# A gated mix of sliding-window attention and a routed expert: the written order of all five engines exchanged for another

## The chip, the cores and the metric

The kernel runs on one core of a Trainium2 chip. The metric is the time of one execution on the device in microseconds (us); the time of a kernel is the median of its runs.

The core's engines work side by side, each through its own list of instructions in order: TensorE (PE, matmuls; PEld is its weight load), ScalarE (ACT), VectorE (DVE), GpSimd (POOL) and SyncE (SP), whose list here is nothing but DMA issues. They wait for each other on semaphores.

## The reference

Input x is 2048 rows of 512 (bfloat16). It is used three times and mixed:

```python
g = _sigmoid((x * gate_w).sum(-1, keepdims=True))
# a: 32 heads of 16; row i sees rows i-255 .. i
mask = (idx[:, None] - idx[None, :] >= 0) & (idx[:, None] - idx[None, :] < W)
a = softmax(where(mask, q @ k.T * Dh ** -0.5, -1e9)) @ v, heads joined, @ wo
# b: the 8 rows of largest x @ w_r go through a gated network of width 1792
y = (_silu(x_sel @ w_gate) * (x_sel @ w_up)) @ w_down * sigmoid(r_sel)
b = x, with y added at the 8 rows
return g * a + (1 - g) * b
```

(The lines of a and b are put together from the reference's; q, k, v come from x @ wqkv.)

## The kernel before

**Tiling.** Heads go in four groups c = 0 to 3 of eight heads (128 columns). For each group `proj` makes Q, K and V of each quarter tc of the rows (512 rows) on PE: eight matmuls over half the contraction each, four on one half of the array and four on the other (L628; the first quarter of group 0 uses the whole array, L621). `q_tail`, `k_tail` and `v_tail` bring them out of PSUM: a cast (L575) on DVE or ACT; for K four products with a head mask into `Kbd` (L587), for V a transpose (L603) and two products into `Vbd` (L607).

**Units.** The scores are made in 156 units (`unit`): 128 of four matmuls (two blocks of 32 keys) and 28 of sixteen (L658), on two PSUM banks in turn. One exponential on ACT per unit (L669) writes the probabilities into the ring `PT`, and one small product with a triangle mask (L680), on DVE or POOL, cuts the edge. `pv` multiplies probabilities and V for 128 rows (L699; one operation is eight matmuls of 34 columns), in batches of up to four blocks of rows that share the PSUM tile `psO`. `norm` ends a batch: reciprocal (L726), scale by g (L738), product (L742) into `On`, then a transposing DMA into `OT` (L772), or, in the two last batches, a transposing matmul (L759) and a copy (L764 on ACT, L767 on DVE). Only then may the next batch write `psO`.

**Output.** `outp(a)` multiplies 128 rows of `OT` by wo (L793, tail L790), adds (1 - g) * b (L798; the last block on ACT, L796) and sends them out (L801).

**Expert.** `z_item`, `router`, `ffn` and `ffd` make the gate, find the eight rows, and put them through the network (L873, 112 matmuls of 8 columns; L915). Their weights come by DMA in 35 pieces, each gated on one exponential.

**End.** Three DVE operations test the first 480 columns of the reciprocals `RC` (L1041, L1042, L1043), three more the last 32; a matmul sums the results (L1048), DVE writes `flag` (L1051), every engine loads it (L1181) and branches (L1183) past a general path that is there for other inputs.

**The order.** Nothing of the order follows from the text of these functions. `add` and `dma` only collect operations, numbered as they come; `Sched.schedule` then takes each engine's list from `ORDER` (the gated weight pieces have negative numbers), and an operation that may run on two engines (`alt`) runs on the one whose list it stands in. `BANK` says for each PSUM item which of the two `psG` banks it takes, and which half of the array comes first. `FILL` puts idle matmuls ahead of a unit: a value under 16 is that many pairs on `psO`, which wait for the last norm; 17 and 33 are one matmul on bank 0 or 1 of `psG`. `emit` works out the semaphores from the dependences.

Numbers that the steps below use:

| number | operation |
|---|---|
| 0, 65 to 74 | zero operand of the first idle matmuls (L458), and those ten (L534) |
| 15, 16, 17 | load of the first columns of wk, wq, wv (L489) |
| 24, 25, 26 | transposing load of XT rows 0-383, 384-511, 512-1023 (L483) |
| 18 to 21 | permutation of the first V weights (L495) |
| 75-78, 84-87 | K of rows 0-127, Q of rows 0-383 |
| 79, 80-83 | the cast of that K, its four Kbd pieces |
| 553 to 566 | first half of the expert's network (L873) |
| 1696, 1697, 1698 | last norm |
| 1710, 1721, 1728, 1737 | output sums 12, 13, 14 and 15 |
| 1670, 1699; 1671, 1700 | the transposing matmuls of the two last batches; their copies |
| 1739-1741, 1742-1744 | test of 480 columns of RC, of the last 32 |
| 1745, 1746 | sum of the tests on PE, flag |

Of the kernel before, what the change touches and what calls it, by code (L numbers as in the profile page):

```python
# [39 lines left out]

FILL = {}
FILLN = 240
ORDER = {}
BANK = ""

# [15 lines left out]
class Sched:  # L61
# [64 lines left out]
    def add(self, eng, fn, r=(), w=(), due=0.0, occ=100.0, lat=None, half=2, cls="", item=None, ss=None, nm=1, cw=0, alt=None):  # L126
# [4 lines left out]
        if eng == "pe":  # L131
            op.cw = float(cw)
            op.so = max(1.03 * occ, 0.834 * cw * (2 if half in (0, 1) else 1))
            if ss is not None:
                op.fill = FILL.get(self.nfill, 0)
                self.nfill += 1
# [211 lines left out]
def fast_path(nc, sem_es, flag, A_x, A_wqkv, A_wo, B_x, B_w_r, B_w_gate, B_w_up, B_w_down, gate_w, out):  # L348


    with ExitStack() as es:
# [706 lines left out]
        if SHOW is not None:  # L1058
# [44 lines left out]
FILL = {15: 2, 18: 1, 39: 1}  # L1103
BANK = ("2020230020200202202000222030202200220022000202022202000022002222002022002")
ORDER = {
# [40 lines left out]
    "act": [16, 22, 23, 15, 88, 93, 104, 13, 114, 122, 119, 129, 157, 160, 169, 172, 151, 185, 201, 215, 224, 227, 286, 236, 248, 251, 260, 263, 276, 295,   # L1146
# [929 lines left out]
```

## Time and profile before

| | |
|---|---|
| median of 3 runs (lowest, highest) | 181.54 us (181.53, 181.98) |
| the profiled execution | 182.41 us |
| its span, first to last instruction | 179.8 us |
| mean granted PE clock | 0.971 |
| HBM read, written | 11.81 MB, 4.20 MB |

The span begins with loads and tables until the first projection at 7.8 us; from 11.9 to 167 us the exponentials run; the last output product ends at 172.8 us, and the flag and the branch close the span. A row of the chain of waits or of the timeline has its start and its length in us, then the engine, the line and the tiles; a group has busy time, the mean of one in ns, and the idle time of the engine ahead of it with what ended it.

### The profile page before, as it was taken

How to read it: one execution, taken by the hardware profiler on the slowest of the kernel's cores; microseconds unless marked ns; L12 is line 12 of the kernel's file. 1: busy time of each engine (PE TensorE's matmuls, PEld its weight loads, DVE VectorE, ACT ScalarE, POOL GpSimd, SP SyncE). 2: the span in 40 equal slices, each digit the busy share in tenths (PEclk: the TensorE clock that was granted, in tenths of full speed). 3: DMA queues.
4: the chain of work that ended last, by engine and by line, in shares of the span. 5: the costliest groups of instructions: out<-in, count | busy, mean ns of one | idle time of the engine just before them, and what ended most of it. 6: DMA issues, size and time to landing. Idle time of an engine off the chain costs nothing.

```text
span 179.8 us, 10017 instructions
## 1 busy us (share of the span) xinstructions
PE 156.8 (87%) x4568; PEld 109.7 (61%) x4568; DVE 123.4 (69%) x343; ACT 137.6 (77%) x168; POOL 73.0 (41%) x118
## 2 busy tenths in 40 slices
PE   5599997999979989899888999699999989979850
PEld 1245674877556686675566658378768667856520
DVE  7075999898486539565765868577796785657760
ACT  2056988999988968888878959799999988957120
POOL 2052078992937476334525317633135336001000
PEclk9969999999999996999999999999999999999996
DMA  4994061656563574634451412120231025546420
GB/s 99 217 216 114 12 188 36 135 134 147 122 157 106 150 122 139 146 107 114 129 117 57 117 36 62 55 71 4 60 93 33 5 54 156 155 129 113 145 88 16
DMA packets 35745, 18.68 MB, mean 104 GB/s; under 512 B 27616, under 2 KB 35568, under 8 KB 35568
## 3 DMA queue, kind: packets, MB, share of 16 engines
q1 hardware_dynamic: 34560, 17.71, 41.2%
q8 instruction: 36, 0.59, 1.4%
q10 hardware_dynamic: 1072, 0.26, 0.7%
q14 instruction: 13, 0.11, 0.2%
q0 software_dynamic: 64, 0.02, 0.0%
HBM read 11.81 MB, written 4.20 MB: 89 GB/s over the span
## 4 chain that ended last, share of the span: by engine, by line
PE 63%; issue 10%; ACT 10%; DVE 10%; DMA 3%; SPq 1%; POOL 0%; POOLq 0%; DVEq 0%
PE f_psO L699 19%; PE f_psG L628 17%; PE f_psS L658 16%; ACT f_PT L669 9%; PE f_psG L793 5%; DMA f_XT<-in_A_x_dram 3%; DVE f_On L742 2%; PE f_psG L621 2%; PE f_psG L873 2%; PE f_psG L915 2%; DVE f_RC L726 1%; DVE f_PT L523 1%; DVE f_RG L738 1%; DVE f_VT L603 1%; SPq L483 1%
## 5 line engine op out<-in xcount | busy, mean ns | idle before, releaser
L669 ACT ACTIVATE f_PT<-f_psS 128x1024 bf16<-128x1024 f32 (+3 forms) x156 | 133.0, 917 | 20.6 <-PE f_psS L658 19.7
L658 PE MATMUL f_psS<-f_QT,f_Kbd 64*128 64x256 bf16 (+3 forms) x960 | 65.9, 225 | 4.2 <-issue 2.2
L699 PE MATMUL f_psO<-f_Vbd,f_PT 64*128 64x34 bf16 x2880 | 60.8, 174 | 5.5 <-issue 2.7
L680 POOL TENSOR_TENSOR f_PT<-f_PT,f_MK 128x128 bf16<-128x128 bf16 (+1 forms) x65 | 38.0, 593 | 65.1 <-ACT f_PT L669 62.2
L699 PEld LDWEIGHTS f_psO<-f_Vbd,f_PT 64*128 64x128 bf16 x2880 | 55.5, 93 | 14.2 <-DVE f_On L742 4.8
L628 PE MATMUL f_psG<-f_XT,f_W 64*128 64x512 bf16 x360 | 62.7, 380 | 0.1
L658 PEld LDWEIGHTS f_psS<-f_QT,f_Kbd 64*128 64x128 bf16 x960 | 32.4, 94 | 21.6 <-ACT f_PT L669 6.0
L680 DVE TENSOR_TENSOR f_PT<-f_PT,f_MK 128x128 bf16<-128x128 bf16 (+1 forms) x91 | 22.3, 271 | 6.5 <-ACT f_PT L669 6.2
L628 PEld LDWEIGHTS f_psG<-f_XT,f_W 64*128 64x128 bf16 x360 | 20.6, 94 | 8.5 <-PE f_psG L628 0.5
L793 PE MATMUL f_psG<-f_wo,f_OT 64*128 64x512 bf16 x112 | 21.2, 376 | 0.0
L587 POOL TENSOR_SCALAR f_Kbd<-f_Kr,f_hm 128x512 bf16<-128x512 bf16 (+2 forms) x11 | 16.2, 1479 | 12.1 <-DVE f_W L495 7.6
L587 DVE TENSOR_SCALAR f_Kbd<-f_Kr,f_hm 128x512 bf16<-128x512 bf16 (+2 forms) x57 | 20.1, 378 | 1.3 <-ACT f_Kr L575 1.1
L607 POOL TENSOR_SCALAR f_Vbd<-f_VT,f_pb 128x512 bf16<-128x512 f32 x17 | 12.7, 750 | 14.3 <-DVE f_VT L603 9.4
L575 DVE CAST f_Kr<-f_psG 128x512 bf16<-128x512 f32 (+1 forms) x14 | 9.2, 660 | 10.7 <-PE f_psG L628 6.3
L798 DVE SCALAR_TENSOR_TENSOR f_outt<-f_xr,f_omg_f,f_psG 128x512 bf16<-128x512 bf16 x15 | 11.2, 745 | 6.3 <-PE f_psG L793 4.5
L575 DVE CAST f_QT<-f_psG 128x512 bf16<-128x512 f32 (+1 forms) x16 | 10.5, 659 | 6.4 <-PE f_psG L628 4.8
L603 DVE STREAM_TRANSPOSE f_VT<-f_psG 128x512 f32<-128x512 f32 x16 | 11.4, 713 | 2.5 <-PE f_psG L628 1.3
L726 DVE RECIPROCAL f_RC<-f_psO 128x32 f32<-128x32 f32 (+1 forms) x17 | 5.8, 343 | 9.3 <-PE f_psO L699 6.7
L742 DVE TENSOR_TENSOR f_On<-f_psO,f_RG 128x512 bf16<-128x512 f32 (+1 forms) x17 | 11.2, 659 | 0.5
L607 DVE TENSOR_SCALAR f_Vbd<-f_VT,f_pb 128x512 bf16<-128x512 f32 x15 | 8.3, 553 | 0.0
L793 PEld LDWEIGHTS f_psG<-f_wo,f_OT 64*128 64x128 bf16 x112 | 6.9, 93 | 2.2 <-issue 0.2
L534 PE MATMUL f_psS<-f_RC 128*128 128x512 bf16 x10 | 4.0, 584 | 2.1 <-DVE f_qi L469 2.1
(104 smaller groups left out, 69.9 us busy)
## 6 DMA issues: line engine op xcount, KB each, us to landing
f_xc<-in_A_x_dram SPq DMA_DIRECT2D x8, 256.0 KB, 3.3
f_xr<-f_xc SPq DMA_DIRECT2D x16, 128.0 KB, 2.6
out_dram<-f_outt SPq DMA_DIRECT2D x16, 128.0 KB, 2.2
f_big<-in_B_w_gate_dram SPq DMA_DIRECT2D x8, 224.0 KB, 3.7
f_big<-in_B_w_up_dram SPq DMA_DIRECT2D x8, 224.0 KB, 3.3
f_OT<-in_B_w_down_dram SPq DMA_DIRECT2D x4, 256.0 KB, 4.0
f_W<-in_A_wqkv_dram SPq DMA_DIRECT2D x2, 384.0 KB, 3.7
f_xr<-in_B_w_down_dram SPq DMA_DIRECT2D x2, 256.0 KB, 3.7
```

The source lines that it names most:

```text
L575: return e.copy(out=o, in_=i) if e is nc.scalar else e.tensor_copy(out=o, in_=i)
L587: add("dve", lambda e, h=h: e.tensor_scalar(out=Kbd[:, sl, a // 32:(a + n) // 32, h, :], in0=Kr[:, kr, a:a + n].rearrange("p (a k) -> p a ...
L603: add("dve", lambda e: e.transpose(out=VT[:], in_=psG[:, it.r, :]), item=it, w=[("VT", vb)], occ=630, due=due, cls="ev")
L607: add(VENG, lambda e, o=o, i=i, b=b: e.tensor_scalar(out=o, in0=i, scalar1=pb_[:, b:b + 1], scalar2=1.0, op0=ALU.mult, op1=ALU.mult), r=[( ...
L628: return e.matmul(psG[:, it.r, 0:n], W[P, kc, which, 128 * c:128 * c + 128], XT[P, kc, 512 * tc + a:512 * tc + a + n], start=(k8 == 0), st ...
L658: ins[s] = e.matmul(psS[:, sb2 + s, n * k:n * k + n], Kbd[P, kslot[(c, kb // 16)][0], kb % 16].rearrange("p h k -> p (h k)"), QT[P, c % 2, ...
L669: add("act", lambda e: e.activation(out=oa, in_=ia, func=ACT.Exp, scale=0.25), r=[("S", i % 2)], w=pk_ + [("ex", i)], occ=2 * nk * n * 0.8 ...
L680: add(eng, lambda e: e.tensor_tensor(out=v, in0=v, in1=m, op=ALU.mult), r=MKR + pk_, w=pk_, occ=cost[eng], due=at(i + 1), cls="mk", alt=(o ...
L699: ins[r] = e.matmul(psO[:, r, 68 * ji + 34 * s:68 * ji + 34 * s + 34], PT[P, s, o0:o0 + 128], Vbd[P, c % 2, s, kb, :], start=(kb == kbs[0] ...
L742: add("dve", lambda e: e.tensor_tensor(out=o, in0=i0_, in1=i1_, op=ALU.mult), r=["O", "RG"], w=[("On", ob, 0), ("On", ob, 1)], occ=60 + 12 ...
L793: return e.matmul(psG[:, it.r, :], OTrun(c, a, 1)[P], wo[P, c, :], start=(k8 == 0), stop=(k8 == 7), tile_position=(64 * x, 0), skip_group_ ...
L798: add("dve", lambda e: e.scalar_tensor_tensor(out=outt[:, xs, :], in0=xr[:, xs, :], scalar=omg_f[:, a:a + 1], in1=psG[:, it.r, :], op0=ALU ...
```

## The change

Three tables are replaced: `FILL`, `BANK` and all five lists of `ORDER`. The operations themselves, 1786 of them, are the same. 119 stand in another engine's list: 80 masks (49 from DVE to POOL, 31 back), 17 Kbd pieces (6 to POOL, 11 to DVE), 15 Vbd products (7 to POOL, 8 to DVE) and 7 casts (5 from DVE to ACT, 2 back). The idle matmuls inside the stream go from 8 to 15. The diff, cut to the lines that are spoken of:

```diff
-FILL = {15: 2, 18: 1, 39: 1}
-BANK = ("2020230020200202202000222030202200220022000202022202000022002222002022002")
+FILL = {13: 33, 15: 3, 18: 1, 37: 33, 39: 1, 53: 17, 61: 1}
+BANK = ("2020220020220002032022002203202000022202222200002200022002022002202020202")
 ORDER = {
-    "pe": [65, 66, 67, 68, 69, 70, 71, 72, 73, 74, 84, 85, 86, 87, 75, 76, 77, 78, 140, 89, 90, 91, 92, 98, 99, 100, 101, 103, 113, 106, 107, 108, 109, 
...
-           490, 491, 509, 510, 511, 512, 531, 532, 504, 641, 533, 534, 535, 619, 536, 543, 544, 622, 553, 554, 555, 556, 557, 558, 559, 560, 631, 643, 561, 
...
-           1720, 1705, 1691, 1692, 1693, 1694, 1695, 1706, 1707, 1708, 1709, 1670, 1699, 1724, 1725, 1726, 1727, 1732, 1733, 1734, 1735, 1736, 1745, 1748],
-    "act": [16, 22, 23, 15, 88, 93, 104, 13, 114, 122, 119, 129, 157, 160, 169, 172, 151, 185, 201, 215, 224, 227, 286, 236, 248, 251, 260, 263, 276, 295, 
...
-    "dve": [5, 49, 55, 14, 45, 0, 10, 12, 62, 7, 46, 9, 11, 61, 8, 53, 18, 6, 48, 79, 20, 80, 82, 141, 58, 83, 97, 19, 54, 21, 56, 95, 102, 96, 110, 59, 
...
-           1604, 1595, 1565, 1607, 1499, 1614, 1615, 1616, 1510, 1642, 1648, 1645, 1657, 1660, 1627, 1667, 1668, 1669, 1677, 1638, 1686, 1689, 1721, 1696, 
-           1697, 1698, 1710, 1671, 1742, 1728, 1739, 1740, 1741, 1743, 1744, 1746, 1750],
...
-    "sp": [17, 25, 24, 26, 27, 28, 30, 496, 29, 497, 498, 499, -1, 31, -5, -2, 183, -3, -7, 274, 502, -4, -10, -8, -11, -12, -13, -9, -6, -15, -16, -14, 
...
+    "pe": [65, 66, 67, 68, 69, 70, 71, 72, 73, 75, 76, 77, 78, 74, 84, 85, 86, 87, 89, 90, 91, 92, 98, 99, 100, 101, 103, 113, 106, 140, 107, 108, 109, 
...
+           681, 490, 491, 509, 510, 511, 512, 619, 531, 610, 553, 554, 555, 556, 557, 558, 622, 559, 560, 561, 631, 532, 533, 643, 562, 563, 564, 565, 566, 
...
+           1715, 1716, 1690, 1691, 1692, 1693, 1694, 1695, 1717, 1718, 1719, 1720, 1670, 1699, 1724, 1725, 1726, 1727, 1732, 1733, 1734, 1735, 1736, 1745, 
+           1748],
+    "act": [15, 22, 16, 23, 79, 88, 93, 104, 114, 119, 122, 129, 157, 160, 169, 151, 195, 172, 185, 201, 215, 224, 227, 236, 248, 251, 260, 263, 276, 295, 
...
+    "dve": [14, 5, 6, 10, 8, 59, 0, 11, 55, 58, 12, 64, 56, 62, 54, 9, 83, 51, 53, 18, 7, 21, 81, 82, 49, 60, 19, 20, 45, 57, 46, 47, 102, 97, 95, 94, 52, 
+           141, 48, 96, 110, 111, 61, 115, 120, 139, 123, 112, 50, 130, 150, 291, 495, 152, 170, 153, 154, 155, 198, 196, 197, 199, 211, 212, 246, 180, 
...
+           1401, 1574, 1577, 1576, 1578, 1479, 1575, 1284, 1486, 1487, 1488, 1553, 1731, 1499, 1591, 1514, 1581, 1565, 1412, 1604, 1614, 1615, 1616, 1510, 
+           1739, 1740, 1627, 1667, 1741, 1668, 1689, 1669, 1638, 1710, 1696, 1697, 1742, 1698, 1721, 1671, 1743, 1728, 1744, 1746, 1750],
...
+    "sp": [24, 25, 17, 26, 27, 28, 31, 499, 497, 29, 498, 496, 30, -1, -3, 183, -5, -4, -6, -7, -2, -9, -10, -11, -8, 502, -13, -12, -14, -15, 274, 368, 
...
```

More of the change, by code (lines that the diff above doesn't have):

```diff
@@ L1102 @@
 GATE = [8, 10, 12, 15, 17, 20, 22, 24, 27, 29, 32, 34, 36, 39, 41, 44, 46, 49, 52, 55, 58, 61, 64, 67, 47, 50, 53, 56, 59, 62, 65, 74, 75, 77, 78]
-FILL = {15: 2, 18: 1, 39: 1}
-BANK = ("2020230020200202202000222030202200220022000202022202000022002222002022002")
+FILL = {13: 33, 15: 3, 18: 1, 37: 33, 39: 1, 53: 17, 61: 1}
+BANK = ("2020220020220002032022002203202000022202222200002200022002022002202020202")
 ORDER = {
[40 rows of a table removed]
-    "act": [16, 22, 23, 15, 88, 93, 104, 13, 114, 122, 119, 129, 157, 160, 169, 172, 151, 185, 201, 215, 224, 227, 286, 236, 248, 251, 260, 263, 276, 295,
[6 rows of a table removed]
-    "dve": [5, 49, 55, 14, 45, 0, 10, 12, 62, 7, 46, 9, 11, 61, 8, 53, 18, 6, 48, 79, 20, 80, 82, 141, 58, 83, 97, 19, 54, 21, 56, 95, 102, 96, 110, 59,
[12 rows of a table removed]
-    "pool": [4, 1, 2, 44, 81, 3, 94, 63, 112, 123, 212, 170, 186, 225, 216, 287, 289, 228, 33, 249, 237, 306, 296, 37, 307, 35, 319, 310, 36, 322, 32, 34,
[7 rows of a table removed]
[41 rows of a table added]
+    "act": [15, 22, 16, 23, 79, 88, 93, 104, 114, 119, 122, 129, 157, 160, 169, 151, 195, 172, 185, 201, 215, 224, 227, 236, 248, 251, 260, 263, 276, 295,
[6 rows of a table added]
+    "dve": [14, 5, 6, 10, 8, 59, 0, 11, 55, 58, 12, 64, 56, 62, 54, 9, 83, 51, 53, 18, 7, 21, 81, 82, 49, 60, 19, 20, 45, 57, 46, 47, 102, 97, 95, 94, 52,
[11 rows of a table added]
+    "pool": [44, 4, 63, 1, 2, 80, 105, 158, 161, 173, 186, 216, 213, 225, 33, 202, 306, 237, 228, 3, 277, 307, 32, 38, 397, 34, 343, 42, 39, 319, 346, 35,
[8 rows of a table added]
 }
```

117 rows, old and new, of the table ORDER are left out of this document.

## Prediction

> **What bounds the kernel now.** I read the page first, the shares of the engines and the chain:
>
> ```profile
> span 179.8 us, 10017 instructions
> PE 156.8 (87%) x4568; PEld 109.7 (61%) x4568; DVE 123.4 (69%) x343; ACT 137.6 (77%) x168; POOL 73.0 (41%) x118
> PE 63%; issue 10%; ACT 10%; DVE 10%; DMA 3%; SPq 1%; POOL 0%; POOLq 0%; DVEq 0%
> q8 instruction: 36, 0.59, 1.4%
> ```
>
> The reader is to see that TensorE (PE) is the bound: 87% busy, and 63% of the chain. So the change is worth what it saves in PE's idle time, in PE's slow clock, and at the two ends where PE has nothing to do yet or any more. I look for these four. The waits come next (total, times, longest):
>
> ```profile
> PEld f_psS L658 <- ACT f_PT L669: 6.0, 22, 0.5
> PEld f_psO L699 <- DVE f_On L742: 4.8, 9, 2.1
> POOL f_PT L680 <- ACT f_PT L669: 62.2, 34, 12.4
> ```
>
> Inside the stream PE waits for two things that the program orders: a score bank that the exponentials have not freed (6.0 us in 22 small pieces), and the norm of a batch of outputs (4.8 us in 9 pieces). POOL waits for ACT most of its time, so it has room. The third kind of idle time has no releaser. In the chain, in order of time, these are the gaps called "issue" (start, length):
>
> ```profile
> 52.75 0.96 issue
> 74.14 0.61 issue
> 82.83 0.34 issue
> 87.46 0.54 issue
> 91.93 0.62 issue
> 147.57 0.71 issue
> 159.36 1.13 issue
> ```
>
> With one of 0.39 at 65.42 they are 5.3 us. What they are is told by the window between two neighbours (length; busy time and count of PE, PEld, DVE, ACT, POOL; then clock, DMA share, GB/s):
>
> ```profile
> 83.17:87.46 4.29, 4.26 (x128) 2.85 (x128) 3.67 (x11) 3.86 (x5) 2.05 (x4) 1.00 0.62 159
> ```
>
> Between these two gaps lie exactly 128 + 128 = 256 PE instructions. The q8 row has 36 packets of 0.59 MB together, 16 KB each, and 4568 + 4568 instructions over 36 are 254: a packet is a page of 256 instructions. So PE waits where a page ends and the next has not come. Gap to gap is 4.6 and 4.5 us (82.83, 87.46, 91.93): a page that PE could work through in less than about 4.4 us is held up. All 36 pages at 4.4 us are 158 us, so this floor lies close under the whole stream, and what is saved inside it may come back as a page wait.
>
> **The change, part by part.** Nothing is computed anew; the same 1786 operations stand in other orders.
>
> *Start.* SP's queue now begins with operation 24 (384 rows of XT), then 25 (128 rows), then 17 (V weights); before it was 17, 25, 24. The chain's first steps and the first PE work:
>
> ```profile
> 0.81 0.47 SPq L489
> 1.34 1.31 SPq L483
> 2.70 5.00 DMA f_XT<-in_A_x_dram
> 7.84 0.82 PE f_psG L621 x4
> 2.08 4.04 PE L534 MATMUL f_psS<-f_RC 128*128 128x512 bf16 x10 [2.08 <-DVE f_qi L469]
> 11.89 1.02 ACT L669 ACTIVATE f_PT<-f_psS 128x1024 bf16<-128x1024 f32 x1 [0.52 <-PE f_psS L658]
> 14.41 2.10 ACT L669 ACTIVATE f_PT<-f_psS 128x1024 bf16<-128x1024 f32 x2 [0.52 <-PE f_psS L658]
> ```
>
> The 5.00 us now begin at 0.81 and not at 2.70: XT lands at 5.8 instead of 7.7, so 1.9 us are to be had. Late next are the idle matmuls in front. Their operand (memset L458, operation 0) is now seventh on DVE instead of sixth, behind two that wait for POOL's iota; I estimate a start at 2.5 instead of 2.08, and nine at 4.04 / 10 each end at 6.2. So the first K matmul comes at about 6.2 and not 7.84: 1.6 us. After that DVE has a wait within its queue: 18 (a quarter of the V weights' permutation) stands ahead of two of the first Kbd's pieces, and its load is now third on SP, behind both transposes (1.9 us behind the first's issue at their 0.47 and 1.31). I estimate that it lands by 8 and the first Kbd is whole near 9; the third exponential (14.41 before) needs the second Kbd, with fifteen small DVE operations ahead of it. At 2.24 / 12 = 0.19 us each (the first window below) that is 2.8 us, with the waits for their inputs near 13. I take **-1.5** (from -0.5, if the weights land late, to -2.4, what the first exponential gains).
>
> PE's clock bears on this too:
>
> ```profile
> 8.99:12.40 3.41, 3.08 (x18) 1.55 (x19) 2.24 (x12) 1.17 (x3) 1.65 (x3) 0.50 1.12 212
> 63.60:67.00 3.40, 3.01 (x115) 2.71 (x111) 0.76 (x3) 2.11 (x3) 2.10 (x5) 1.00 0.39 86
> 67.00:70.43 3.43, 3.43 (x73) 2.08 (x71) 2.78 (x11) 2.71 (x5) 1.75 (x5) 0.50 0.67 213
> ```
>
> The clock is halved twice, 3.41 us each. The first half-clock stretch follows the idle time before 7.84. With PE busy from 2.5 on I expect it gone; its gain is inside the -1.5. The Trainium skill ("TensorE: Matmul & The Clock Gate", part "What's actually happening") speaks against that: the activity window is 3.41 us long and free-running, so where it lies against the first matmul is chance. The lengths here agree; by the rule the start would gain only its -0.5 in some executions, and the sum below would be 1.0 higher.
>
> *The slow clock at the router's network.* The second stretch follows 112 matmuls of 8 columns at L873 (written as fourteen operations). Before, 13 of them stood in one page with no PV; now 7 and 8 stand in two pages with 7 and 5 PV operations between, and one idle matmul at unit 53. In the half-clock window PE made 73 matmuls, against 115 in the window ahead; I price that stretch at 1.2 us. Whether the mixing is enough no row shows: 0 to -1.2, I take the middle, **-0.6**.
>
> *PV and norms.* Between the last PV of a batch and the first of the next DVE needs reciprocal, scale and product:
>
> ```profile
> 159.08 0.36 DVE L726 RECIPROCAL f_RC<-f_psO 128x32 f32<-128x32 f32 x1 [0.19 <-PE f_psO L699]
> 159.69 0.69 DVE L742 TENSOR_TENSOR f_On<-f_psO,f_RG 128x512 bf16<-128x512 f32 x1
> 77.61 0.86 PE f_psG L628 x8
> ```
>
> That is 1.3 us, some 1.6 with the two hand-overs. I counted the other PE work written into each of the 16 boundaries, at 0.11 us per projection or output matmul (0.86 / 8) and twice that per score unit. Before, seven boundaries hold under 1.4 us; after, two (0.9 and 1.3). What is missing to 1.6 sums to 3.0 before and 1.5 after. The 4.8 us of waits should halve, -2.4; the page floor takes part of it back. I take half, **-1.2** (0 to -2.4).
>
> *Pages.* PE has 4565 useful and idle matmuls, now 7 more (FILL), so pages stay about 36. At the same prices, with 0.14 us per PV operation (eight pairs), 8 pages hold under 3.6 us of work before, 9 after; what is missing to 4.0 sums to 6.2 before and 7.3 after. By that the gaps do not shrink: **+0.6** (from +2, if every shortfall is paid, to -4, if the order fits the fetch better than my prices see). The Trainium skill ("Runtime: NRT & Kernel Launch", part "Instruction fetch mechanics") has page steps mostly hidden; the 5.3 us of gaps disagree. By that rule this term would be 0 and the sum 0.6 lower.
>
> *Idle matmuls and engine swaps.* Seven more idle matmuls:
>
> ```profile
> L545 PE MATMUL f_psO<-f_ident 64*128 64x240 bf16 x8 | 1.2, 265 | 0.9 <-DVE f_On L742 0.9
> L669 ACT ACTIVATE f_PT<-f_psS 128x1024 bf16<-128x1024 f32 x116 | 112.2, 1025 | 13.2 <-PE f_psS L658 12.3
> L575 ACT CAST f_Kr<-f_psG 128x512 bf16<-128x512 f32 x2 | 1.2, 583 | 0.0
> L680 POOL TENSOR_TENSOR f_PT<-f_PT,f_MK 128x128 bf16<-128x128 bf16 x53 | 24.4, 466 | 55.6 <-ACT f_PT L669 52.7 <-DVE f_MK L518 2.7
> L680 DVE TENSOR_TENSOR f_PT<-f_PT,f_MK 128x128 bf16<-128x128 bf16 x75 | 16.5, 239 | 6.5 <-ACT f_PT L669 6.2
> ```
>
> At 1.2 / 8 = 0.15 us they are 1.05 us in the open and nothing in a wait: **+0.5**. Of 119 operations on another engine, masks go 49 to POOL and 31 back, evictions net 3 to ACT. ACT gets 3 x 0.58 = 1.7 us; its 13 us of waits for scores cover that mostly: **+0.3** (0 to +1.7). The masks give POOL net 18 x 0.47 = 8.4 us and take 18 x 0.24 = 4.3 from DVE; POOL's waits cover it: 0.
>
> *Tail.* Now the clearest part:
>
> ```profile
> 171.72 1.03 PE L790 MATMUL f_psG<-f_wo,f_OT 128*128 128x512 bf16 x4
> 160.00:170.00 10.00, 9.07 (x259) 6.18 (x259) 6.84 (x20) 5.20 (x8) 0.46 (x1) 1.00 0.58 127
> 172.43 0.40 DVE L1041 TENSOR_SCALAR f_scr<-f_RC 128x480 f32<-128x480 f32 x1
> 174.58 0.24 PE L1048 MATMUL f_psO<-f_ones_f,f_okc 128*1 128x1 f32 x4 [1.83 <-DVE f_okc L1043]
> 174.86 0.15 DVE L1051 TENSOR_SCALAR flag<-f_psO 1x1 int32<-1x1 f32 x1 [0.33 <-PE f_psO L1048]
> L1183 PEldq COMPARE_BRANCH  x1: 4177/4177/4177, 175.6 to 175.6; - x1
> L1183 SPq COMPARE_BRANCH  x1: 58/58/58, 175.8 to 175.8; - x1
> ```
>
> PE ends its last output product at 172.75 and then waits 1.83 us for DVE, which only now tests 480 columns of RC (1739 to 1741). Then come the flag (175.01) and PE's branch, which takes 4.18 us and is the last thing in the span. After the change 1739 to 1741 stand six to nine microseconds earlier, among norms and output sums, where DVE is busy 6.84 of 10 us; only the 32-column test is left. Against it: one small test (0.17 us) now lies inside the last norm, and output sum 13 behind it; I give 0.25. So the flag comes 1.83 - 0.25 = **1.6 us** earlier, at 173.4, and the branch ends 1.6 earlier. Its cover is SP, which must see the last output land: it branches at 175.8, still before PE's branch would end (178.2). Should the branch wait for what SP does, this term is 0.
>
> Sum: -1.5 - 0.6 - 1.2 + 0.6 + 0.5 + 0.3 - 1.6 = **-3.5 us**. The profiled execution took 182.41 (span 179.80 and 2.61 around it); that gives 178.9 by its own time. The median of the runs is 181.54, so by that **178.0 us**, -1.9%.
>
> **The rivals.**
>
> A. The new order fits the pages better than my count sees, and most of the 5.3 us goes. For: gaps stand at known places and a written order can put long matmuls there. Against: 9 short pages against 8. It gives 3.9 us less than the forecast's page term: about 174.2.
>
> B. The page floor takes back what the norms and the clock save (+1.8), and the start gives only -0.5 (+1.0): 178.0 + 2.8 = 180.8, little but faster. For: 36 x 4.4 = 158 us. Against: only eight pages of 36 end in a gap now.
>
> C. Slower: masks on POOL. One takes 0.47 us there and 0.24 on DVE, with three more behind it in POOL's queue. POOL's order of units 42 to 55 holds 12.4 us (10.8 before) beside 14 exponentials, and every PV of a batch waits for its last mask. If that adds 0.35 us at each of 16 batches, 5.6 us are lost: 178.0 + 5.6 = 183.6. It decides from 0.25 us per batch on. Against it stands POOL's 62.2 us of waiting for ACT.
>
> D. Nothing measurable: half of C with B, 181 to 182.
>
> **How the numbers follow.** Less than about 0.3% (0.5 us) can't be told from no change here: faster means below 181.0, slower above 182.1. Forecast, 176.5 to 179.6: 0.52. A, below that: 0.15. B, up to 181.0: 0.13. D: 0.08. C: 0.12. So faster 0.80, same 0.08, slower 0.12. Range: from half of A, 175.0, to the middle of D, 181.5, which leaves out about 0.06 below and 0.14 above.
>
> **What would show it.** Start: the first L621 matmul near 6.2, the first exponential before 10.5, the third near 13, a granted clock of 1.00 from 9 to 12.4. Tail: no 1.83 us before L1048, the branch ending 4.2 us after the flag. Norms: PEld waits for f_On under 3 us. Clock: no half-clock window at L873. Pages: the sum of issue gaps of 0.3 us and more, 5 to 6.5. Wrong would I be if PE waits for L680 by the microsecond (C), if the issue gaps fall below 2 us (A), or if the span's end follows SP and not PE.

## The result and the profile after

| | before | after |
|---|---|---|
| median of the runs | 181.53 us (179.03 to 181.98, 4 runs) | 172.62 us (172.00 to 172.96, 4 runs) |
| ratio to before | | 0.955, 95% interval 0.945 to 0.965 |
| profiled execution, its span | 182.41, 179.8 us | 172.88, 171.3 us |

The change is worth 8.9 us here, more than twice the 3.5 that were forecast, and the time lies below the range. A median is of all runs and a ratio of the fast ones alone (within 1.5% of the kernel's fastest), so the two can differ. The page of the kernel after, in the lines that were shown of before (engines and PE's clock in 40 slices):

```profile
span 171.3 us, 10022 instructions
...
PE 157.3 (92%) x4575; PEld 108.2 (63%) x4575; DVE 119.7 (70%) x328; ACT 138.3 (81%) x171; POOL 67.3 (39%) x130
...
PEclk9999999999999957999999999999999999999997
...
q8 instruction: 36, 0.59, 1.5%
```

PE is busy for as long as before (157.3 against 156.8 us) in a span 8.5 us shorter: what went is idle time of PE. The waits, before's idle time put down to "issue" first, then after's (engine, what waited; total, times, longest):

```profile
PE f_psO L699 <- issue: 2.7, 4, 1.0
...
PE f_psS L658 <- issue: 2.2, 3, 1.1
...
PE f_psG L873 <- issue: 0.7, 2, 0.4
```

```profile
POOL f_PT L680 <- ACT f_PT L669: 79.8, 37, 8.0
...
PEld f_psS L658 <- ACT f_PT L669: 10.6, 35, 0.7
...
PEld f_psO L699 <- DVE f_On L742: 3.5, 6, 1.2
...
PE f_psG L793 <- DVE f_outt L798: 1.2, 1, 1.2
...
PE f_psO L699 <- issue: 0.6, 1, 0.6
...
PE f_psG L873 <- issue: 0.3, 1, 0.3
```

Before had 5.8 us of gaps of 0.1 us and more at nine page ends; after has one, 0.60 us at 152.63. (In both, these gaps stand where the number of the PE instruction leaves 193 when divided by 256.) No idle piece of PE of 0.1 us or more ends with a mask (before has one, 0.24 us).

The start of the kernel after in the timelines of PE and ACT (start, length, what, idle time before it):

```profile
2.39 3.49 PE L534 MATMUL f_psS<-f_RC 128*128 128x512 bf16 x9 [2.39 <-DVE f_pb L472]
5.71 0.39 PE L621 MATMUL f_psG<-f_XT,f_W 128*128 128x128 bf16 x4
```

```profile
8.61 1.94 ACT L669 ACTIVATE f_PT<-f_psS 128x1024 bf16<-128x1024 f32 x2 [0.48 <-PE f_psS L658]
11.62 2.81 ACT L669 ACTIVATE f_PT<-f_psS 128x1024 bf16<-128x1024 f32 x3 [1.08 <-PE f_psS L658]
```

The first exponential comes at 8.61 and not at 11.89, the third at 11.62 and not at 14.41. PE's clock is full from 5.20 to 59.82 us.

The tail, in the timeline of all engines and the instructions of the branch's line (L1184 in this kernel):

```profile
164.99 1.03 PE L790 MATMUL f_psG<-f_wo,f_OT 128*128 128x512 bf16 x4
...
165.95 0.24 PE L1048 MATMUL f_psO<-f_ones_f,f_okc 128*1 128x1 f32 x4
...
166.23 0.15 DVE L1051 TENSOR_SCALAR flag<-f_psO 1x1 int32<-1x1 f32 x1 [0.35 <-PE f_psO L1048]
```

```profile
L1184 PEldq COMPARE_BRANCH  x1: 4133/4133/4133, 167.1 to 167.1; - x1
L1184 SPq COMPARE_BRANCH  x1: 58/58/58, 169.1 to 169.1; - x1
```

L1048 follows the last output product at once. PE's branch, 4.13 us from 167.1, again ends the span, and SP branches at 169.1, well inside it.

The expert's network, in windows (length; busy time and count of PE, PEld, DVE, ACT, POOL; clock, DMA share, GB/s):

```profile
56.40:59.82 3.42, 3.07 (x122) 2.56 (x115) 1.35 (x5) 3.08 (x5) 3.12 (x4) 1.00 0.35 95
59.82:63.22 3.40, 3.40 (x99) 2.54 (x98) 0.44 (x2) 2.28 (x3) 3.07 (x6) 0.50 0.53 111
63.22:66.64 3.42, 3.32 (x132) 2.11 (x130) 1.67 (x5) 3.10 (x6) 2.82 (x5) 0.50 0.00 0
```

Two windows are at half clock, where before had one.

### The profile page after: what moved, and what is told of

The parts are those of the page before. It is cut to its first block, busy times and chain, and to the rows that moved or that the text cites. A ratio compares the mean times of both kernels' runs of the same rounds, so it can differ in the third digit from the quotient of the medians.

```text
span 171.3 us, 10022 instructions
## 1 busy us (share of the span) xinstructions
PE 157.3 (92%) x4575; PEld 108.2 (63%) x4575; DVE 119.7 (70%) x328; ACT 138.3 (81%) x171; POOL 67.3 (39%) x130
## 5 line engine op out<-in xcount | busy, mean ns | idle before, releaser
L680 POOL TENSOR_TENSOR f_PT<-f_PT,f_MK 128x128 bf16<-128x128 bf16 (+1 forms) x83 | 41.5, 513 | 83.7 <-ACT f_PT L669 79.8
L628 PE MATMUL f_psG<-f_XT,f_W 64*128 64x512 bf16 x360 | 65.8, 379 | 0.3
L699 PEld LDWEIGHTS f_psO<-f_Vbd,f_PT 64*128 64x128 bf16 x2880 | 54.3, 93 | 10.3 <-DVE f_On L742 3.5
L699 PE MATMUL f_psO<-f_Vbd,f_PT 64*128 64x34 bf16 x2880 | 58.4, 174 | 2.2 <-DVE f_On L742 1.2
L793 PE MATMUL f_psG<-f_wo,f_OT 64*128 64x512 bf16 x112 | 22.9, 376 | 1.2 <-DVE f_outt L798 1.2
L680 DVE TENSOR_TENSOR f_PT<-f_PT,f_MK 128x128 bf16<-128x128 bf16 (+1 forms) x73 | 19.5, 285 | 4.7 <-ACT f_PT L669 4.5
L587 DVE TENSOR_SCALAR f_Kbd<-f_Kr,f_hm 128x512 bf16<-128x512 bf16 (+2 forms) x62 | 20.9, 374 | 1.9 <-ACT f_Kr L575 1.6
L607 POOL TENSOR_SCALAR f_Vbd<-f_VT,f_pb 128x512 bf16<-128x512 f32 x16 | 11.6, 729 | 2.5 <-DVE f_VT L603 2.3
L575 DVE CAST f_Kr<-f_psG 128x512 bf16<-128x512 f32 x12 | 8.2, 686 | 3.4 <-PE f_psG L628 3.2
L587 POOL TENSOR_SCALAR f_Kbd<-f_Kr,f_hm 128x512 bf16<-128x512 bf16 (+1 forms) x6 | 8.5, 1420 | 5.1 <-ACT f_Kr L575 5.1
L793 PEld LDWEIGHTS f_psG<-f_wo,f_OT 64*128 64x128 bf16 x112 | 7.6, 93 | 4.2 <-DVE f_outt L798 1.9
```

The lines of the kernel that those rows point to most:

```text
L575: return e.copy(out=o, in_=i) if e is nc.scalar else e.tensor_copy(out=o, in_=i)
L587: add("dve", lambda e, h=h: e.tensor_scalar(out=Kbd[:, sl, a // 32:(a + n) // 32, h, :], in0=Kr[:, kr, a:a + n].rearrange("p (a k) -> p a ...
L607: add(VENG, lambda e, o=o, i=i, b=b: e.tensor_scalar(out=o, in0=i, scalar1=pb_[:, b:b + 1], scalar2=1.0, op0=ALU.mult, op1=ALU.mult), r=[( ...
L628: return e.matmul(psG[:, it.r, 0:n], W[P, kc, which, 128 * c:128 * c + 128], XT[P, kc, 512 * tc + a:512 * tc + a + n], start=(k8 == 0), st ...
L680: add(eng, lambda e: e.tensor_tensor(out=v, in0=v, in1=m, op=ALU.mult), r=MKR + pk_, w=pk_, occ=cost[eng], due=at(i + 1), cls="mk", alt=(o ...
L699: ins[r] = e.matmul(psO[:, r, 68 * ji + 34 * s:68 * ji + 34 * s + 34], PT[P, s, o0:o0 + 128], Vbd[P, c % 2, s, kb, :], start=(kb == kbs[0] ...
```

## The experiments

In the edits, numbers are operations in an engine's list. A ratio is to the kernel before in the same rounds on the same chip. The rounds were made in several jobs on several chips, so medians are compared within a job. Numbered exponentials and units count from 0.

**The tail alone (b_tail).**

```diff
 before, "dve": ...
-1742, 1728, 1739, 1740, 1741, 1743
+1510, 1739, 1740, ... 1667, 1741, ... 1742, 1728, 1743
```

> The kernel before, with the three operations that test 480 columns of RC (1739 to 1741) moved to the places that they have in the changed kernel. Theory 'flag': the end follows the flag, so the 1.83 us ahead of L1048 goes and the span falls by 1.5 to 1.9 us, to about 178.1; nothing else moves. Rival 'output': the end follows the last output's landing, and the span stays within 0.4 us of 179.8.

178.63 us against 180.92, ratio 0.992 (0.987 to 0.997). From the start of the last exponential to the end of the span it takes 11.9 us, against 13.3 to 13.8 in four executions of before. The end follows the flag. The profiled span, though, is 172.9 us, 6.9 below before's and not the 1.5 to 1.9 foretold: this execution has 1.2 us of page gaps where before's first had 5.8, and starts earlier, neither of which the edit was meant to touch. One profile of an edit shows more than the edit. The reverse:

**The tail undone (a_tailback).**

```diff
 after, "dve": ...
-1510, 1739, 1740, 1627, 1667, 1741, 1668 ... 1728, 1744
+1510, 1627, 1667, 1668 ... 1728, 1739, 1740, 1741, 1744
```

> The kernel after with the tests 1739 to 1741 back behind 1728 on DVE, as before. Theory 'flag' (PE waits for the last test, and the end follows the flag): a wait of 1.6 to 1.9 us ahead of L1048 again, median 1.0 to 1.9 us above the kernel after (less than 1.9 if the last output sums come earlier without the tests ahead of them). Theory 'SP' (the end follows the landing of the last output): within 0.4 us of it.

175.40 us, against 174.52 for the kernel after in the same job (below): 0.9 more, a little under the 1.0 to 1.9 foretold, and less than the runs of either kernel differ among themselves (174.19 to 177.25, 171.53 to 176.66). What shows the effect is the timeline, where the wait is back:

```profile
165.77 1.03 PE L790 MATMUL f_psG<-f_wo,f_OT 128*128 128x512 bf16 x4
168.42 0.24 PE L1048 MATMUL f_psO<-f_ones_f,f_okc 128*1 128x1 f32 x4 [1.62 <-DVE f_okc L1043]
```

**The head of SP's queue alone (b_sphead), and undone (a_sphead).**

```diff
 before, "sp":
-17, 25, 24, 26
+24, 25, 17, 26
 after, "sp":
-24, 25, 17, 26
+17, 25, 24, 26
```

> The kernel before, with only the first three transfers of SP's queue in the order of the changed kernel (24, 25, 17). Theory 'XT': the first L621 matmul starts when XT lands, 1.5 to 2.0 us earlier (near 6.2), and the span falls by about as much as the third exponential comes earlier, 1 to 2 us. Rival 'lists': the early part hangs on DVE's and ACT's lists as well, so the third exponential gains under 0.7 us of the 2.8 that the changed kernel gains there, and the span under 0.7.

> The kernel after with the head of SP's queue as it was (17, 25, 24). Theory 'loads' (the transposes' place gives 1.8 us of the start, DVE's and PE's new order the rest): exponentials 1.5 to 2.2 us later than in the kernel after from unit 4 on, median 1.5 to 2.2 us above it. Theory 'all by the loads': 3 us or more. Theory 'floor' (the fetch of pages bounds the stream, so a late start is made up by shorter page gaps): exponentials late at unit 16, but less than 0.6 us at unit 100, and the median within 0.5 us of the kernel after.

178.21 against 180.92 us (ratio 0.991, 0.984 to 0.997); undone, 177.46 against 174.52 for after, and a ratio to before of 1.000 (0.994 to 1.007): with the old head no gain over before's runs in that job was left. ACT's timelines, first of before with the new head, then of after with the old one:

```profile
9.68 1.02 ACT L669 ACTIVATE f_PT<-f_psS 128x1024 bf16<-128x1024 f32 x1 [0.22 <-PE f_psS L658]
```

```profile
11.78 1.94 ACT L669 ACTIVATE f_PT<-f_psS 128x1024 bf16<-128x1024 f32 x2 [0.52 <-PE f_psS L658]
14.19 2.81 ACT L669 ACTIVATE f_PT<-f_psS 128x1024 bf16<-128x1024 f32 x3 [0.47 <-PE f_psS L658]
```

In these pairs the new head alone takes exponential 16 from 29.78 to 27.97 (-1.8), and the old one puts it from 26.46 to 29.01 (+2.6). But the clock differs between the executions as well. The same twelve matmuls, first in after, then in after with the old head:

```profile
6.15 1.78 PE L621 MATMUL f_psG<-f_XT,f_W 128*128 128x384 bf16 x12
```

```profile
7.98 3.19 PE L621 MATMUL f_psG<-f_XT,f_W 128*128 128x384 bf16 x12
```

They start 0.16 us apart in the one and 0.32 in the other, where the first record of a full clock is at 11.74 us (after: 5.20). The slow clock makes these twelve alone 1.4 us longer, and that is inside the 2.6. In the profiles with before's lists of PE and the first DVE operations, exponential 16 starts at 28.6 to 30.1 with the old head (five) and at 28.0 to 28.4 with the new one (three), 1.2 us earlier in the mean. So the loads are worth 1.2 to 2.6 us of the 3.3 by which it moved; how the rest divides between the order on PE and DVE and the clock was not tested.

**Both (b_both).** The two edits of before together.

> The kernel before with both tried parts of the change: the three tests earlier on DVE and the head of SP's queue (24, 25, 17). Theory 'sum' (start and tail are on the path and independent): 1.8 + 1.5 us below before, and what is left to the kernel after (some 2 to 4 us) is the order in between. Theory 'floor' (what one end gains, the pages take back): within 1 us of the better of the two alone, that is 1.6 to 2.6 us below before.

176.59 us against 180.63, ratio 0.981 (0.974 to 0.988): 4.0 less by the medians. The ratios of the two alone multiply to 0.983, so the two add up; the profile still has 0.9 us of the wait ahead of L1048. A form of the kernel after in the same job (a_shift64, below) took 173.65: some 3 us are left for the order in between.

**Where the pages end (a_shift, b_shift, a_shift64).** Idle matmuls in front are cut into pieces, with the columns unchanged, so that each page ends 126 (64) PE instructions earlier in the work; the edit of a_shift and b_shift, with pieces of 64 columns:

```diff
-for _ in range(NWARM):
-    add("pe", warm, ...
+for n in range(NWARM):
+    add("pe", (lambda e: warm(e, 8)) if n < 9 else warm, ...
```

> The changed kernel, with nine of the ten first idle matmuls cut into eight pieces of 64 columns each: 63 matmuls and 63 weight loads more, so every page of 256 PE instructions ends 126 instructions earlier in the program; the columns streamed are the same. Theory 'places': the order was fitted to the places where pages end, so gaps at page ends come back, three or more, 1.5 to 4 us in all, and the span rises to 173 to 175. Rival 'spread': the order only spreads the PV operations or keeps the queue filled, wherever pages end; at most two such gaps, and the span stays within 0.8 us of 171.3.

> The kernel before, with the same 63 idle pieces more in front. Theory 'places': its order had nothing to do with page ends, so the gaps fall elsewhere but sum to about the same, 4 to 7.5 us, and the span stays within 1.5 us of 179.8. Rival 'spread': the same prediction for the sum, but gaps stand in the same stretch of the program (47 to 97 us) as before. If instead the gaps go below 2 us, page ends are not what they are.

> The kernel after with 64 more PE instructions among the idle matmuls in front (four 512-column ones cut into 8, one into 4, one into 2 pieces; the same columns), so that every page ends 64 instructions earlier in the order. Theory 'places' (the new order fits where its pages end): the gaps come back at other places as with 126 instructions, 3.5 us or more of them, median 2 to 4.5 us above the kernel after. Theory 'luck': 0.6 to 3.1 us of gaps as in the four profiles of unshifted forms of it, and the median within 1.2 us of it, plus 0.4 us for the pieces.

a_shift: 176.91 us against 180.92, ratio 0.981 (0.974 to 0.989). Its "issue" waits, where L701, L875 and L917 are the L699, L873 and L915 of the kernel after:

```profile
PE f_psO L701 <- issue: 2.8, 5, 1.0
...
PE f_psG L917 <- issue: 1.6, 1, 1.6
...
PE f_psG L875 <- issue: 0.4, 1, 0.4
```

The gaps were back, 4.3 us at six other page ends, as "places" foretold. But a_shift64 had 2.3 us of gaps and 173.65 us (ratio 0.968, 0.958 to 0.977), as a form without a shift might. b_shift: 182.00 against 180.92, ratio 1.010 (0.987 to 1.034), 5.5 us of gaps at eleven ends, as both theories had it. That where the pages end decides was not confirmed.

**All of SP's order (b_spall).** Before with the whole SP list of after.

> The kernel before with the whole list of SP (all its loads and stores) of the kernel after; PE's pages hold what they held. Theory 'places' (page gaps come from which instructions share a page): like the kernel before with the new head of SP alone, 178.2 us within 0.7, fetches beginning later than 1.1 us after PE enters a page, 2 us or more of page gaps. Theory 'contention' (data transfers beside the fetch make it late, and the new order of loads moved them out of the way): median 175 to 177 us, fetches beginning within 1.0 us in the mean up to 100 us, page gaps under 1.2 us.

179.47 against 179.31 us, ratio 1.009 (1.004 to 1.015): the time missed both theories. Page gaps of 2.2 us and a fetch that begins 1.24 us late in the mean are what "places" said, and "contention" missed these too. The gain at the start is lost again in a wait of 1.7 us of L793 for an output sum:

```profile
PE f_psO L1048 <- DVE f_okc L1043: 1.8, 1, 1.8
PE f_psG L793 <- DVE f_outt L798: 1.7, 1, 1.7
```

**The same kernels again (a_again, b_again; b_look2, b_look3, a_look2, a_look3).**

> The kernel after, unchanged, once more, beside before in the same rounds. Theory 'order' (the new order gives PE's sequencer a lead over the fetch in every execution): median 172 to 173.5 us, highest less than 2 us above the lowest, gaps at page ends below 1.2 us in the profile, and the fetch of a page beginning 1.0 us or less after PE enters the page ahead of it in the mean. Theory 'luck' (how late the fetch comes differs by execution, as it does in before, and four executions happened to be good): median 174 to 176 us, 3 us or more between lowest and highest, 2 to 5 us of page gaps.

> The kernel before, unchanged, with a profile of another execution. Theory 'order' (its pages hold what makes PE wait, in every execution): 4.5 to 6.5 us of gaps at page ends, at the same pages as in the first profile (four in a row from 83 to 97 us). Theory 'luck' (how late a page is fetched differs from execution to execution): 1 to 3 us, as in the kernels before with only DVE's or only SP's list changed (1.2 and 2.1 us), the four in a row not all there, and a span shorter by about the difference.

> The kernel before, a third profiled execution (the first two: 5.76 and 4.65 us of page gaps of 0.1 us and more). Theory 'order': 4 us or more again. Theory 'luck': anything from 1.2 (as with three DVE operations of the tail moved) to 5.8 us.

> The kernel after, a third profiled execution (the first two: 0.60 and 1.01 us). Theory 'order': below 1.5 us again. Theory 'luck': up to 3 us and more.

b_look3 and a_look3 had the same expectations. After took 174.52 us (171.53 to 176.66, 6 runs) beside 179.31 for before: by these medians the gain was 4.8 us there, not 8.9. (After's quickest run, 171.53, lies 6.1 below the median of before's five quickest, 177.60.) Either gain would lie inside the forecast's range. The unchanged before took 180.83 beside 180.63 (ratio 1.011, 0.990 to 1.032). The single runs b_look2 and b_look3 took 178.38 and 179.56 us, a_look2 and a_look3 172.37 and 177.03. Two chains of before in order of time, the "issue" steps, first of b_again and then of b_look2:

```profile
63.99 0.65 issue
...
72.70 1.00 issue
...
81.77 0.64 issue
...
86.69 0.54 issue
...
91.16 0.62 issue
...
146.53 0.68 issue
...
158.25 0.33 issue
```

```profile
51.75 0.29 issue
...
79.82 0.28 issue
...
142.77 0.97 issue
...
154.78 0.34 issue
```

It is the same program on the same data, and the row from 81 to 92 is there in one and gone in the other, except for 0.28 (and 0.26 at 84.4, which the chain leaves out). PE's time in four profiled executions of each kernel, added up from the records of its instructions:

| us | before (1st to 4th) | mean | after (1st to 4th) | mean | difference |
|---|---|---|---|---|---|
| span | 179.8, 178.2, 174.8, 177.2 | 177.5 | 171.3, 169.4, 170.8, 175.0 | 171.6 | -5.9 |
| page gaps | 5.8, 4.7, 2.4, 2.7 | 3.9 | 0.6, 1.0, 0.8, 2.7 | 1.3 | -2.6 |
| idle in the first 300 instructions | 4.1, 4.8, 3.9, 3.9 | 4.2 | 3.0, 3.0, 3.0, 2.9 | 3.0 | -1.2 |
| other idle pieces of 0.1 us and more | 7.3, 7.2, 6.8, 7.0 | 7.1 | 4.2, 2.6, 3.2, 3.3 | 3.3 | -3.7 |
| busy, with the branch | 161.8, 160.6, 160.9, 162.6 | 161.5 | 162.4, 161.5, 162.6, 164.9 | 162.8 | +1.4 |

(The rest, shorter pieces and the wait for the flag, is +0.4.) So both theories have a share: the sums overlap (2.4 and 2.7 us), and in the mean after has 2.6 us less. Of the 5.2 us by which the first two profiles differ in page gaps, half or more is owed to the executions that were profiled (and perhaps to their chips). Six further profiles leave PE's own list as it was: before's in b_tail, b_sphead, b_spall and b_both (1.2, 2.1, 2.2 and 3.4 us of page gaps), after's in a_sphead and a_tailback (3.1 and 2.0). With them the means are 3.1 us in eight and 1.7 in six, a difference of only 1.4, in ranges (1.2 to 5.8, 0.6 to 3.1) that overlap widely. How much of it the new order owns is thus not shown.

**The clock (a_clk).**

```diff
-FILL = {..., 53: 17, 61: 1}
+FILL = {..., 51: 24, 53: 23, 61: 1}
```

> The kernel after with idle matmuls of 240 columns around the router's network (8 at score unit 51, where there were none, and 7 instead of 1 at unit 53). [...] Theory 'columns': both windows of the network then hold over 6,000, no window or one is halved there instead of two, exponentials from unit 60 on 1 to 2.5 us earlier than in the kernel after; 14 idle matmuls at 0.10 us cost 1.4 us of that, so the median falls by 0.3 to 1.5 us. Theory 'weights' (the gate goes by something else, such as rows times columns): two halved windows remain and the median rises by 1 to 1.8 us.

The windows of the network in this kernel, to be held against the three above:

```profile
56.22:59.63 3.41, 3.20 (x111) 2.48 (x108) 1.10 (x4) 1.83 (x4) 2.69 (x4) 1.00 0.41 135
59.63:63.05 3.42, 3.42 (x112) 2.75 (x109) 1.16 (x3) 2.73 (x4) 1.99 (x3) 1.00 0.42 116
63.05:66.46 3.41, 3.08 (x128) 2.49 (x126) 0.87 (x4) 2.91 (x4) 3.15 (x4) 1.00 0.04 8
```

The clock stays full, yet the time is 173.47 us (171.81 to 175.15; ratio 0.968, 0.959 to 0.977), as that of a_shift64 in the same job (173.65). Held against the exponentials of the kernel after, 1.0 us is lost between units 48 and 52 and 0.1 is made up by unit 60, which comes 1.3 us later, where it was foretold 1 to 2.5 us earlier: the idle matmuls cost what the clock gives. Nor does a count of columns tell which windows are followed by a halved one: the window from 59.63 held 5,248 and not over 6,000, and none followed; in the kernel after none followed 5,232 (from 8.6 us) and one did 4,568 (from 56.40), in a_shift none followed 4,096 (from 99.1), and in b_sphead one did 6,436 (from 63.1). So this kernel beats before, but was not shown to beat after.

## Why the prediction was wrong in size and right in direction

**Pages (+0.6): the step that failed.** It said that by the count of short pages the gaps do not shrink, and put them 0.6 us up. In the profiled pair they shrank by 5.2 us, in the mean of four executions each by 2.6, in the mean of all fourteen profiles whose PE list is one of the two, unchanged, by 1.4. The count had the wrong sign, but hardly mattered: taken from the two traces, page gaps left out, 5 pages of before and 4 of after are under 3.6 us (foretold 8 and 9), and what is missing to 4.0 is 5.3 and 4.9 us (foretold 6.2 and 7.3). What failed is the step from short pages to gaps: a short page is only held up if its fetch begins late. By the trace's DMA records q8 begins to fetch the next page a while after PE has entered a page: in the first 100 us 1.71, 1.50, 1.38 and 1.27 us in the mean of the four executions of before, and 1.02, 1.15, 0.84 and 1.17 in those of after. A fetch takes about 1.0 us, and where PE waited in before's first profile, the page's first instruction ran 1.3 to 1.5 us after the landing. That makes 1.7 + 1.0 + 1.4 = 4.1 us for a page in the first profile of before, and 3.4 with 1.0: many pages lie between the two. My "4.4 us" was the floor of one execution, taken for one of the chip. The Trainium skill ("Runtime: NRT & Kernel Launch", part "Instruction fetch mechanics") says that the next page is fetched while the current one runs, which the records show, and that the step is mostly hidden: true of after's first profile (0.6 us), not of before's (5.8).

What makes the fetch begin earlier in after is open, and its mean lateness does not give the gaps by itself: b_shift had 1.13 us of it and 5.5 us of gaps, b_tail 1.23 and 1.2. It isn't the page ends alone (a_shift64), nor SP's order alone (b_spall). Lateness and the share of the DMA engines that the other queues hold in the 2.5 us after a page is entered go together in all eight profiles of the unchanged kernels (correlations of 0.3 to 0.6 within an execution), so data beside the fetch remains a rival; a kernel with less of it was not tried.

**Start (-1.5): right in kind, half the size.** The first K matmul came at 5.71, foretold for 6.2, the first exponential before 10.5, the clock at 1.00; but the third exponential came at 11.62 and not at 13. For the most part it was the chain on DVE that I priced too high. DVE's timeline after:

```profile
7.42 0.13 DVE L495 COPY f_W<-f_outt 128x128 bf16<-128x128 bf16 x1
...
7.64 0.42 DVE L587 TENSOR_SCALAR f_Kbd<-f_Kr,f_hm 128x128 bf16<-128x128 bf16 x2
...
9.22 0.77 DVE L587 TENSOR_SCALAR f_Kbd<-f_Kr,f_hm 128x384 bf16<-128x384 bf16 x3
...
10.47 0.32 DVE L587 TENSOR_SCALAR f_Kbd<-f_Kr,f_hm 128x384 bf16<-128x384 bf16 x1
```

The V weights were there by 7.42 (estimate: 8), the first Kbd whole at 8.06 (9), the second at 10.79 (13). The 300th PE instruction ends at 15.82 and not at 19.07, 3.3 us earlier; over four executions exponential 16 is earlier by 2.7 (29.6 to 26.8). The full clock is less of a hit than it looks. The half-clock stretch does not belong to before's idle time ahead of the first projection: b_look3 has it (from 9.65 us), but b_again and b_look2 idle there too (1.9 and 0.9 us) and keep a full clock from 7.2 us on. So part of the 3.3 us is the draw of the execution, as the prediction's own objection allowed. Against that, none of the nine profiles with after's order has the stretch at that place and three of nine with before's do, though a_sphead's clock is first full at 11.74 us.

**Clock (-0.6): wrong sign.** Mixing the network with PV spread it over two windows, and two were halved where before had one. Over four executions it is 2, 2, 2 and 3 against 1, 1, 1 and 2. By the price of 1.2 us a window that is +1.2; by a_clk a full clock, bought with idle matmuls, was not shown to gain anything on balance.

**PV and norms (-1.2): right.** PE's other idle time fell by 3.1 us in the pair (7.26 to 4.19) and by 3.7 in the mean of four, of which 1.8 is the tail; 1.3 and 1.9 are left. The idle pieces that a norm ends fell by more (3.2 to 1.5 us in the pair), but after has a new wait of 1.2 us for an output sum. The tell-tale, waits for f_On under 3 us, was missed by a little (3.5).

**Idle matmuls and swaps (+0.8):** PE's busy time rose by 0.5 us with the half clock in it. Masks: nothing, as foretold, so rival C is out.

**Tail (-1.6): right.** The 1.83 us ahead of L1048 went, and from the last exponential to the end it takes 13.6 us before and 11.9 after in the mean of four. Undoing it brought the wait back.

**The rivals.** A's mark (issue gaps below 2 us) was met in three of after's four profiles, and its 174.2 us is near the 173.9 that after's twelve runs give in the mean; that the order "fits the pages", as A said, is not shown. B's page floor did not take the savings back. D's price does not add up: half of C (2.8) on top of B (180.8) is 183.6 and not 181 to 182, and the range's upper end hung on it. Nor can 0.5 us be told apart, as the forecast had it: before's four runs beside the result alone lie 3.0 us apart. With pages at -2.6 and the start at -2.7, each in place of its term, the sum is -7.9 us, 173.6 by the median; with pages alone it is 174.8, just under the range. But the clock term had the wrong sign: with it at +1.2 the sum is -6.1, which is near the -5.9 by which the spans differ in the mean of four, and at 175.4 inside the range. So the miss of the range is a close one, and not steady: after's median lies 4.8 us below before's in a_again's job, those of its forms a_shift64 and a_clk 7.0 and 7.2 in theirs, and 8.9 here.

## What to carry to other kernels

A gap that has no releaser must be seen in several executions before it is priced: here it came to 2.4 to 5.8 us for one program, and both "a floor" and "a gain" read from one profile were half luck or more. The same holds for an edit: compare it with several executions of the kernel that it was made from, and look at the clock of each. Undo each part of a large reordering by itself, at both ends, for there the path is plain (loads' order 1.2 to 2.6 us, a late test 0.9 to 2.3); what lies in between is then known as a remainder. A transfer's place in a queue is worth what all that follows it gains, so follow the start to the third or fourth step, with durations from the rows, before taking a margin.

## What the runs showed that was not expected

- One program's page gaps differ by more than 3 us from execution to execution, in which of the pages are held up too.
- The lateness of a page's fetch, 0.8 to 1.7 us in the mean, tells the sums of the unchanged kernels apart better than the pages' lengths do; in the edited ones it does not.
- Two windows at half clock in the network's stretch, 6.8 us, were not shown to cost more than 14 idle matmuls of 240 columns (some 1.4 us at 0.10 each). Why so little was not tested.
